# Weight-block sums: the low parts move to GpSimd, the first sum waits, and the order is computed with later landings

## The chip, the cores and the metric

The kernel runs on one NeuronCore of a Trainium2 chip. The metric is the device time of one execution in microseconds (us); shorter is better. The engines are called as the profile calls them: PE is TensorE (matmuls, with PEld for its weight loads), DVE is VectorE, ACT is ScalarE, POOL is GpSimd, and SP is SyncE, whose queue issues the DMAs (SPq).

## What is computed

The reference is windowed attention with eight memory keys, and a feed-forward network on its result:

```python
# 4 batches x 8 heads x 768 queries, head size 64; chunks of 32 queries see 16 keys to the left, 8 to the right
scores = scale * np.matmul(q_c, k_full.transpose(0, 1, 3, 2))
a = np.exp(scores - np.max(scores, axis=-1, keepdims=True))
a = a / (np.sum(a, axis=-1, keepdims=True) + 1e-09)
out[:, :, c_start:c_end] = np.matmul(a, v_full)
...
# 3072 tokens x 512; w_in is 512 x 2048, w_out is 2048 x 512
h = x @ w_in
r = np.maximum(h, 0.0)
g = s * (r * r) + b
return (g @ w_out).astype(np.float32)
```

## The kernel before

**Number format.** Every large matrix product is done as three fp32r products: a value is held as a high part (a rounded copy) and a low part (the value less its high part), and low*high, high*low and high*high are added in PSUM. So each operand costs one ACT copy for the high part and one subtraction for the low part.

**Stages.** The 3072 tokens are eight chunks of 384. Chunks 0 to 3 go through the network as written: `hidden(u)` (line 564) multiplies one 128-wide slice of w_in with the chunk (12 matmuls, L571), ACT makes relu, square and affine of it and the high part gH (L579 to L582), DVE the low part gL (L583); `result(u)` (line 588, 9 matmuls, L596) multiplies gL and gH with the slice of w_out. There are 64 such steps u. Chunks 4 to 7 go through the network in pairs by a Strassen scheme (`mix`, `seven` with L769, `rest` with L884), which needs sums of weight blocks. In front of that and between the steps, the attention of each chunk and pair of heads runs: scores on PE (L426), a custom DVE operation for mask and maximum (L493), exp on ACT (L497), the norm on POOL with a reciprocal on DVE in its midst (L506, L508, L509), eight transposes of 32x32 blocks on DVE ("flips", L529), the product with the values on PE (L463).

**Weights.** The 32 slices of w_in and w_out are loaded and converted once from 64-bit words by `weight` (line 536): ACT L546 and L555, DVE L547, L549, L551 and L556. L556 writes the low part. The words come through a ring of four buffers (`words`), which the block sums and the loads of `mix` use later in the same ring, strictly in the order in which they were declared.

**Block sums.** `blocks(side, g)` (line 630) is called 16 times, for w_in (side 0) and w_out (side 1). For two slices it takes high and low together again on POOL (two L637 of 128x512), makes four sums and differences S1 to S4 of 128x256 from them (POOL: two L643, L645, L647), the high part of all four at once on ACT (L650) and their low part on DVE (L651, 128x1024). SP stores the parts to DRAM (L656, issued in the code of `put`), from where `seven` and `rest` stream them back. A block holds four buffers of the ring: `full`, `sums`, `high`, `low`.

**The order.** Nothing is issued in the order in which the Python code runs. `op` collects every operation with its engine, an assumed duration (`HOLD`), a priority and what it reads and writes; `Plan.lay` (line 169) lays them out by greedy list scheduling, and the result is issued as it stands, so each engine's queue has a fixed order. On the chip an instruction waits only for the data that it really uses. In the plan every block sum also depends on `all_w`, the parts of the last slice of either matrix, but the instruction for it reads only its own two slices. Operations marked `lock` on DVE and POOL are never laid over each other in the plan. A load is taken to land `LAND` = 2000 ns after its bytes have passed a wire of `RATE` = 400 bytes per ns.

Of the kernel before, what the change touches and what calls it, by code (L numbers as in the profile page):

```python
# [12 lines left out]
F32R = mybir.dt.float32r  # L13
# [3 lines left out]
ALU = mybir.AluOpType  # L17
# [24 lines left out]
NEARLY = 16  # L42
# [30 lines left out]
            low=475, affine_v=475, rec=120, max=212, flip=449, xlow=470, wlow=365, wjoin=610, wsign=612, out=600,  # L73
            small=300, prod=1062, half=525, gsum=985, gsumv=470, tsumv=850, one=180, chigh=420, scaled=400, add=480, wide=735, vsum=1260, ssum=700, shigh=950, slow=1143, tsum=1800, thigh=735, tlow=880, norm=1010, norm2=1870, wrest=1290, issue=440)
LATE = dict(PE=230, ACT=180, DVE=180, POOL=150, SP=0)
SAME = dict(PE=0, ACT=118, DVE=115, POOL=60, SP=0)
RATE, LAND = 400.0, 2000.0
SLOW, NSLOW = 290.0, 6
FLIGHT = 8
BEGIN = dict(PE=2500.0, ACT=2500.0, DVE=2500.0, POOL=2500.0, SP=800.0)  # L80


class Op:
    __slots__ = ("eng", "hold", "fn", "deps", "outs", "prio", "lock", "vals", "n", "start", "end", "left", "ready", "size", "done")


class Val:
# [55 lines left out]
class Plan:  # L143
# [5 lines left out]
    def op(self, eng, kind, prio, fn, reads=(), writes=(), lock=False, size=0):  # L149
        o = Op()  # L150
        o.eng, o.hold, o.fn, o.prio, o.lock, o.n, o.size = eng, HOLD[kind], fn, prio, lock, len(self.ops), size
        o.deps, o.outs, o.vals = set(), [], []
        for part in reads:
            o.deps.update(part[1])
        for part in writes:
            o.deps.update(part[1])
            o.deps.update(part[2])
        for part in reads:
            part[2].append(o)
        for part in writes:  # L160
            part[1][:] = [o]
            part[2].clear()
        o.vals = list({id(p[0]): p[0] for p in (*reads, *writes)}.values())
        for v in o.vals:
            v.left += 1
        self.ops.append(o)
        return o

    def lay(self, filler=None):

        for o in self.ops:
            o.left, o.ready, o.start = len(o.deps), 0.0, None
            for d in o.deps:
                d.outs.append(o)
        engines = ["PE", "ACT", "DVE", "POOL", "SP"]
        free = dict(BEGIN)
        lock = {"DVE": 0.0, "POOL": 0.0}
        waiting = {e: [] for e in engines}
        ready = {e: [] for e in engines}
        events = sorted(BEGIN.values())  # L180
        wire, flying, sent = 0.0, [], 0
        laid = []
        back = []
        for o in self.ops:
            if not o.left:
                heapq.heappush(waiting[o.eng], (0.0, o.n, o))
        todo = len(self.ops)
        while todo:
            t = heapq.heappop(events)
            while events and events[0] <= t:  # L190
                heapq.heappop(events)
            while back and back[0][0] <= t:
                v = heapq.heappop(back)[-1]
                v.ring.back(v)
            for e in engines:
                while waiting[e] and waiting[e][0][0] <= t:
                    o = heapq.heappop(waiting[e])[2]
                    heapq.heappush(ready[e], (o.prio, o.n, o))
                if free[e] > t:
                    continue  # L200
                if e == "SP":
                    flying = [x for x in flying if x > t]
                    if len(flying) >= FLIGHT:
                        heapq.heappush(events, min(flying))
                        continue
                put, got = [], None
                while ready[e]:
                    x = heapq.heappop(ready[e])
                    o = x[2]
                    new = [v for v in o.vals if v.slot is None and v.ring.tiles is not None]  # L210
                    other = "POOL" if e == "DVE" else "DVE"
                    held = o.lock and e in lock and lock[other] > t

                    if o.lock and e in lock and free[other] <= t and any(y[2].lock and y[:2] < x[:2] for y in ready[other]):
                        put.append(x)
                        continue
                    given = []
                    for v in new if not held else ():
                        if not v.ring.can(v):
                            break  # L220
                        v.ring.give(v)
                        given.append(v)
                    if not held and len(given) == len(new):
                        got = o
                        break
                    for v in reversed(given):
                        v.ring.undo(v)
                    if held:
                        heapq.heappush(events, lock[other])
                    put.append(x)  # L230
                for x in put:
                    heapq.heappush(ready[e], x)
                if got is None:
                    if e == "PE" and filler and filler[0](t):
                        laid.append((t, -1, filler[1]))
                        free[e] = t + HOLD["warm"]
                        heapq.heappush(events, free[e])
                    continue
                o = got
                o.start = t  # L240
                free[e] = t + o.hold
                o.end = free[e] + LATE[e]
                if o.size:
                    wire = max(wire, t) + o.size / (RATE if sent >= NSLOW else SLOW)
                    sent += 1
                    o.end = wire + LAND
                    flying.append(o.end)
                if o.lock and e in lock:
                    lock[e] = free[e]
                laid.append((t, o.n, o.fn))  # L250
                todo -= 1
                heapq.heappush(events, free[e])
                for d in o.outs:
                    d.left -= 1
                    d.ready = max(d.ready, free[e] + SAME[e] if d.eng == e and not o.size else o.end)
                    if not d.left:
                        heapq.heappush(waiting[d.eng], (d.ready, d.n, d))
                        heapq.heappush(events, d.ready)
                for v in o.vals:
                    v.left -= 1  # L260
                    v.done = max(getattr(v, "done", 0.0), o.end)
                    if not v.left and v.ring.tiles is not None:
                        heapq.heappush(back, (v.done, o.n, o.vals.index(v), v))
                        heapq.heappush(events, v.done)
            if not events and todo:
                stuck = [(o.eng, o.prio, [v.kind for v in o.vals if v.slot is None]) for e in engines for _, _, o in ready[e]]
                raise AssertionError(f"the plan is stuck at {t}: {todo} left, {stuck[:12]}")
        self.end = max(o.end for o in self.ops)
        laid.sort(key=lambda x: (x[0], x[1]))
        return laid  # L270
# [3 lines left out]
def body(ctx: ExitStack, tc: tile.TileContext, qkv, w1, w2, out):  # L274
    nc = tc.nc
# [5 lines left out]
    op = plan.op  # L281
# [31 lines left out]
    words = ring("words", 4, [P, 2 * DM], F32)  # L313
# [29 lines left out]
    def warm():  # L343
        nc.tensor.matmul(idle, ones[:, :P], ones, start=True, stop=True)
# [285 lines left out]
    def blocks(side, g, due):  # L630

        fs = (2 * g, 2 * g + 1)
        parts = [[c_w[side, f]["H"], c_w[side, f]["L"]] for f in fs]
        full, sums, high, low = (Val(words) for _ in range(4))
        at = lambda v, i, n=1: v.tile[:, i * 2 * P:(i + n) * 2 * P]
        for k, f in enumerate(fs):
            op("POOL", "vsum", due, lambda k=k, f=f: nc.gpsimd.tensor_tensor(  # L637
                at(full, 2 * k, 2), weight_tile(side, f)[:, 0].bitcast(F32), weight_tile(side, f)[:, 1].bitcast(F32), ALU.add),
               [*parts[k], *all_w], (full[k],), lock=True)
        whole = (full[0], full[1])  # L640
        a12, a21 = (2, 1) if side else (1, 2)
        for i, a, b, how in ((0, a21, 3, ALU.add), (2, 0, a21, ALU.subtract)):
# [5 lines left out]
           (*whole, sums[1]), (sums[3],), lock=True)  # L648
        every = [sums[i] for i in range(4)]
        op("ACT", "shigh", due, lambda: nc.scalar.activation(high.tile.bitcast(F32R), sums.tile, AF.Copy), every, (high[0],))  # L650
        op("DVE", "slow", due, lambda: nc.vector.tensor_tensor(low.tile.bitcast(F32R), sums.tile, high.tile, ALU.subtract),  # L651
           (*every, high[0]), (low[0],), lock=True)
        for n, name in enumerate(BLOCKS):
            unit, q = divmod(ORDER2.index(name) * (NF // 2) + g if side else g * len(BLOCKS) + n, 2)
            dst = (w1s, w2s)[side][unit][:, q]
# [2 lines left out]
            if name in SUMS:  # L658
                i = SUMS.index(name)
                put(lambda i=i: at(high, i), dst[:, 0], (high[0],), 0)  # L660
                put(lambda i=i: at(low, i), dst[:, 1], (low[0],), 1)
            else:
                i, k = int(name[1]) - 1, int(name[2]) - 1
                if side:
# [286 lines left out]

    laid = plan.lay((lambda t: spare and t < 40e3, warm))
    with tc.manual_schedule():
        for _, _, fn in laid:
            fn()


# [37 lines left out]
```

## Time and profile before

| | |
|---|---|
| median of 3 runs | 618.76 us (618.1 to 619.36) |
| the profiled execution | 621.25 us, of which 619.5 us are the span |
| mean granted TensorE clock | 0.997 |
| PE busy | 598.3 us (97%) |
| DVE busy | 456.2 us (74%) |
| ACT busy | 435.1 us (70%) |
| POOL busy | 188.9 us (30%) |

The span runs from the first to the last instruction. Busy shares are means over stages with different limits, so the stages have to be read one by one. In a timeline row, the bracket at the end gives the idle time of that engine just before the row and what ended it. A matmul's end is modelled, so PE shown as busy can still be a little short of its peak.

### The profile page before, as it was taken

The page shows a single profiled execution, that of the slowest core. Times are in us where ns is not written, and L with a number is a line of the kernel's source. Part 1 is how long each engine was busy: PE and PEld are TensorE (multiplying, and loading weights), DVE is VectorE, ACT ScalarE, POOL GpSimd, SP SyncE. Part 2 cuts the span into 40 slices and gives each one's busy share as a digit, 9 for nine tenths or more (in the row PEclk, how much of TensorE's full clock was granted, in tenths as well). Part 3 has the DMA queues.
Part 4 walks back from the last instruction along what each step waited for, and adds up shares of the span by engine and source line. Part 5 has one row for each costly group of instructions (what it writes and reads, how often), then busy time and mean ns, then how long its engine had stood idle before and what let it go on. Part 6 is the DMA issues. An engine that isn't in the chain of part 4 may idle for free.

```text
span 619.5 us, 11570 instructions
## 1 busy us (share of the span) xinstructions
PE 598.3 (97%) x3827; PEld 539.0 (87%) x3831; DVE 456.2 (74%) x1277; ACT 435.1 (70%) x1157; POOL 188.9 (30%) x202
## 2 busy tenths in 40 slices
PE   9999999899999899999999999999999999999996
PEld 5778778788888788887878789999999999999996
DVE  5999899856787877776765778784999544439873
ACT  6999998675766888668585767775765436656562
POOL 4623100568575577683112022321000001110000
PEclk9999999899999999999999999999999999999999
DMA  8934665034887989789435648787878887777871
GB/s 332 404 130 157 204 220 172 1 115 136 275 246 250 304 256 277 253 268 312 123 118 199 219 141 300 250 296 249 266 245 285 292 283 251 243 248 252 274 225 52
DMA packets 68988, 141.28 MB, mean 228 GB/s; under 512 B 6976, under 2 KB 39744, under 8 KB 68928
## 3 DMA queue, kind: packets, MB, share of 16 engines
q1 hardware_dynamic: 68928, 140.54, 68.0%
q8 instruction: 30, 0.49, 0.3%
q14 instruction: 30, 0.25, 0.1%
HBM read 101.71 MB, written 38.80 MB: 227 GB/s over the span
## 4 chain that ended last, share of the span: by engine, by line
PE 56%; DVE 17%; ACT 12%; DMA 8%; issue 3%; SPq 3%; POOL 1%; ACTq 0%; DVEq 0%; POOLq 0%
PE ps L769 19%; PE ps L884 19%; PE ps L596 7%; PE ps L571 5%; ACT t L497 4%; DVE aT L529 3%; DVE gL L583 2%; PE ps L426 2%; DVE w L556 2%; DVE wv L551 2%; PE ps L463 2%; DMA words<-xs 2%; SPq L656 2%; DVE wv L549 2%; ACT words L650 1%
## 5 line engine op out<-in xcount | busy, mean ns | idle before, releaser
L571 PE MATMUL ps<-x,w 128*128 128x384 f32 x768 | 147.7, 339 | 0.5 <-DVE w L556 0.4
L571 PEld LDWEIGHTS ps<-x,w 128*128 128x128 f32 x768 | 135.2, 189 | 7.5 <-DVE w L556 0.9
L596 PE MATMUL ps<-w,gH 128*128 128x512 f32 x384 | 121.3, 397 | 0.2 <-DVE w L556 0.2
L497 ACT ACTIVATE t<-t,nmax 96x128 f32<-96x128 f32 x256 | 100.1, 396 | 29.4 <-DVE nmax L493 28.9
L769 PE MATMUL ps<-again,again 128*128 128x384 f32 x672 | 120.1, 338 | 0.0
L769 PEld LDWEIGHTS ps<-again,again 128*128 128x128 f32 x672 | 117.8, 188 | 1.0
L596 PE MATMUL ps<-w,gL 128*128 128x512 f32 x192 | 79.9, 416 | 13.8 <-DVE gL L583 13.8
L529 DVE STREAM_TRANSPOSE aT<-t 32x256 f32<-32x256 f32 x192 | 83.6, 435 | 11.1 <-POOL t L509 8.4
L509 POOL TENSOR_TENSOR t<-t,rden 96x1024 f32<-96x1024 f32 (+1 forms) x40 | 66.2, 1657 | 67.7 <-DVE rden L508 67.6
L596 PEld LDWEIGHTS ps<-w,gH 128*128 128x128 f32 x384 | 72.6, 189 | 14.7 <-ACT w L555 0.5
L884 PE MATMUL ps<-gH,again 128*128 128x386 f32 x272 | 70.2, 339 | 0.0
L493 DVE CUSTOM_DVE_ANT_0 t<-ps,mask 96x128 f32<-96x128 f32 x256 | 58.7, 281 | 15.3 <-PE ps L426 14.9
L596 PEld LDWEIGHTS ps<-w,gL 128*128 128x128 f32 x192 | 36.1, 188 | 27.2 <-DVE gL L583 19.0
L579 ACT ACTIVATE ps<-ps 128x384 f32<-128x384 f32 x64 | 30.6, 478 | 40.0 <-PE ps L571 39.4
L506 POOL TENSOR_SCALAR rden<-den 96x8 f32<-96x8 f32 (+1 forms) x40 | 12.1, 303 | 145.8 <-ACT t L497 145.2
L583 DVE TENSOR_TENSOR gL<-ps,gH 128x384 fp32r<-128x384 f32 x64 | 35.4, 553 | 24.4 <-ACT gH L582 23.3
L884 PE MATMUL ps<-again,again 128*128 128x386 f32 x264 | 50.1, 338 | 0.0
L497 ACT ACTIVATION_READ_ACCUMULATOR t<-t,nmax 96x1 f32 x256 | 49.8, 195 | 0.0
L884 PEld LDWEIGHTS ps<-gH,again 128*128 128x128 f32 x272 | 49.7, 189 | 0.0
L884 PEld LDWEIGHTS ps<-again,again 128*128 128x128 f32 x264 | 46.9, 189 | 0.0
L637 POOL TENSOR_TENSOR words<-w 128x512 f32<-128x512 f32 x32 | 46.4, 1469 | 0.6
L884 PE MATMUL ps<-gL,again 128*128 128x386 f32 x136 | 46.0, 339 | 0.0
(100 smaller groups left out, 908.2 us busy)
## 6 DMA issues: line engine op xcount, KB each, us to landing
again<-w1s SPq DMA_DIRECT2D x56, 512.0 KB, 4.3
again<-w2s SPq DMA_DIRECT2D x56, 512.0 KB, 4.3
raw<-qkv SPq DMA_DIRECT2D x28, 448.0 KB, 4.1
words<-w SPq DMA_DIRECT2D x22, 512.0 KB, 4.1
w1s<-words SPq DMA_DIRECT2D x64, 128.0 KB, 2.2
w2s<-words SPq DMA_DIRECT2D x64, 128.0 KB, 2.2
v<-qkv SPq DMA_DIRECT2D x28, 256.0 KB, 4.2
w1s<-w SPq DMA_DIRECT2D x24, 256.0 KB, 3.3
```

Source lines behind the costliest of these rows:

```text
L426: nc.tensor.matmul(scv(n)[:, j, :], raw.tile[rows, j * QB:(j + 1) * QB], raw.tile[rows, TOK + j * P:TOK + (j + 1) * P], start=True, stop=True)
L493: op("DVE", "max", a + 0.1, lambda j=j: nc.vector.tensor_tensor_reduce(t.tile[:, n, j, :], scv()[:, j, :], mask[:, kind(j)], -SCALE, 3.0e3 ...
L497: op("ACT", "exp", a + 0.2, lambda j=j: nc.scalar.activation(t.tile[:, n, j, :], t.tile[:, n, j, :], AF.Exp, bias=nmax()[:, j:j + 1], scal ...
L509: op("POOL", "norm2" if wide else "norm", a + 0.25, lambda: nc.gpsimd.tensor_tensor(t.tile[:, heads], t.tile[:, heads], rden().unsqueeze(3 ...
L529: nc.vector.transpose(aT.tile[gg, :, :, cs], t.tile[cs, :, :, gg])
L571: nc.tensor.matmul(h.tile[:, :TOK], weight_tile(0, f)[:, wi, c * P:(c + 1) * P], x.tile[c][:, xi], start=(c == 0 and n == 0), stop=(c == N ...
L579: op("ACT", "relu", u - ahead, lambda: nc.scalar.activation(hp(), hp(), AF.Relu), (), (h[0],))
L583: op("DVE", "low", u - ahead, lambda: nc.vector.tensor_tensor(g.tile[1][:, :TOK], hp(), g.tile[0][:, :TOK].bitcast(F32), ALU.subtract), (h ...
L596: nc.tensor.matmul(acc.tile, g.tile[gi][:, t * P:(t + 1) * P], weight_tile(1, f)[:, wi, :], start=(first and n == 0), stop=(last and n == 2))
L637: op("POOL", "vsum", due, lambda k=k, f=f: nc.gpsimd.tensor_tensor(at(full, 2 * k, 2), weight_tile(side, f)[:, 0].bitcast(F32), weight_til ...
L769: nc.tensor.matmul(bank.tile[:, :TOK], w.tile[:, lo:lo + P], xv.tile[xi][:, kc], start=(not more and kc == 0 and i == 0), stop=(kc == 1 an ...
L884: nc.tensor.matmul(sx(bank), w.tile[:, lo:lo + P], cut.tile[xi], start=(first and k == 0), stop=(last and k == 2), skip_group_check=True)
```

## The change

Three things are changed. The low parts of the block sums are taken by POOL, in two halves of 128x512 and in place (written over `sums`), where DVE did it in one instruction into a fourth buffer; a block then holds three buffers of the ring. The very first block sum gets a real dependency on the instructions that write the low parts of the last slices, so that POOL waits for them on the chip. And in the plan, every load or store after the first 16 is taken to land 1600 ns plus its bytes times (1/190 - 1/400) ns after the wire in place of 2000 ns; the whole order is laid out anew with this.

```diff
@@ constants
 RATE, LAND = 400.0, 2000.0
+HOP, ALONE = 1600.0, 190.0
...
@@ Plan.lay
                     wire = max(wire, t) + o.size / (RATE if sent >= NSLOW else SLOW)
                     sent += 1
-                    o.end = wire + LAND
+                    o.end = wire + (LAND if sent <= NEARLY else HOP + o.size * (1 / ALONE - 1 / RATE))
                     flying.append(o.end)
...
@@ blocks
-        full, sums, high, low = (Val(words) for _ in range(4))
+        full, sums, high = (Val(words) for _ in range(3))
...
-            op("POOL", "vsum", due, lambda k=k, f=f: nc.gpsimd.tensor_tensor(
+            o = op("POOL", "vsum", due, lambda k=k, f=f: nc.gpsimd.tensor_tensor(
                 at(full, 2 * k, 2), weight_tile(side, f)[:, 0].bitcast(F32), weight_tile(side, f)[:, 1].bitcast(F32), ALU.add),
                [*parts[k], *all_w], (full[k],), lock=True)
+            if not (side or g or k):
+                o.after += [p[1][0] for p in all_w[1::2]]
...
         op("ACT", "shigh", due, lambda: nc.scalar.activation(high.tile.bitcast(F32R), sums.tile, AF.Copy), every, (high[0],))
-        op("DVE", "slow", due, lambda: nc.vector.tensor_tensor(low.tile.bitcast(F32R), sums.tile, high.tile, ALU.subtract),
-           (*every, high[0]), (low[0],), lock=True)
+        for k in range(2):
+            op("POOL", "vsum", due + 0.1, lambda k=k: nc.gpsimd.tensor_tensor(
+                at(sums, 2 * k, 2).bitcast(F32R), at(sums, 2 * k, 2), at(high, 2 * k, 2), ALU.subtract), (high[0],), every[2 * k:2 * k + 2], lock=True)
...
-                put(lambda i=i: at(low, i), dst[:, 1], (low[0],), 1)
+                put(lambda i=i: at(sums, i), dst[:, 1], (sums[i],), 1)
...
@@ body, where the laid order is issued
-        for _, _, fn in laid:
-            fn()
+        for _, _, o in laid:
+            if o is None:
+                warm()
+                continue
+            o.ins = o.fn()
+            for x in o.after:
+                tc.add_manual_dep(o.ins.ins, x.ins.ins.name, mybir.DependencyInfo(mybir.DependencyClass.Sync, mybir.DependencyReason.DATA))
```

## Rows read from the trace of the kernel before

**Rows 1.** The page's part 1: busy time, share of the span, instructions.

```profile
PE 598.3 (97%) x3827; PEld 539.0 (87%) x3831; DVE 456.2 (74%) x1277; ACT 435.1 (70%) x1157; POOL 188.9 (30%) x202
```

**Rows 2.** Stretches: length, busy PE, PEld, DVE, ACT, POOL (instructions), PE clock, DMA.

```profile
118.00:285.00 167.00, 159.91 (x1048) 139.14 (x1049) 119.25 (x362) 120.14 (x347) 112.76 (x117) 0.99 0.72 231
285.00:365.00 80.00, 75.47 (x504) 64.79 (x503) 56.32 (x189) 57.67 (x174) 13.62 (x13) 1.00 0.54 180
365.00:615.00 250.00, 249.69 (x1516) 245.99 (x1514) 173.34 (x387) 150.57 (x323) 26.21 (x25) 1.00 0.76 252
```

**Rows 3.** Waits of PE, 121 to 290 us: total, times, longest.

```profile
PE ps L596 <- DVE gL L583: 6.3, 6, 1.8
```

**Rows 4.** Timelines of DVE, POOL and PE around the end of the weight conversions.

```profile
112.57 1.70 DVE L556 TENSOR_TENSOR w<-wv,w 128x512 fp32r<-128x512 f32 x1
114.20 1.78 DVE L551 SCALAR_TENSOR_TENSOR wv<-words,wv 128x512 int32<-128x512 int32 x1
117.25 0.69 DVE L556 TENSOR_TENSOR w<-wv,w 128x512 fp32r<-128x512 f32 x1
...
112.43 3.00 POOL L637 TENSOR_TENSOR words<-w 128x512 f32<-128x512 f32 x2
...
119.93 0.50 PE L596 MATMUL ps<-w,gL 128*128 128x512 f32 x1 [2.46 <-DVE gL L583]
```

**Rows 5.** The stretch right behind the stall; columns as in rows 2.

```profile
120.00:125.00 5.00, 5.00 (x17) 4.28 (x18) 2.01 (x7) 0.92 (x4) 3.17 (x4) 0.66 0.00 0
```

**Rows 6.** The line of the low parts: duration ns min/median/max, first and last start.

```profile
L651 DVE TENSOR_TENSOR words<-words,words x16: 1210/1298/4049, 130.6 to 284.8; 128x1024 fp32r<-128x1024 f32 x16
```

**Rows 7.** DVE's groups, 118 to 285 us: busy us, mean ns, idle before.

```profile
L529 DVE STREAM_TRANSPOSE aT<-t 32x256 f32<-32x256 f32 x93 | 40.5, 435 | 4.2 <-POOL t L509 2.9
L651 DVE TENSOR_TENSOR words<-words,words 128x1024 fp32r<-128x1024 f32 x16 | 32.5, 2033 | 10.1 <-ACT words L650 10.1
```

**Rows 8.** Timelines of ACT, DVE, POOL and PE around one low part.

```profile
179.51 0.49 ACT L582 ACTIVATE gH<-ps 128x384 fp32r<-128x384 f32 x1
...
178.46 3.48 DVE L651 TENSOR_TENSOR words<-words,words 128x1024 fp32r<-128x1024 f32 x1 [0.84 <-ACT words L650]
181.87 0.54 DVE L583 TENSOR_TENSOR gL<-ps,gH 128x384 fp32r<-128x384 f32 x1
...
179.56 3.53 POOL L637 TENSOR_TENSOR words<-w 128x512 f32<-128x512 f32 x2
...
182.46 0.50 PE L596 MATMUL ps<-w,gL 128*128 128x512 f32 x1 [0.87 <-DVE gL L583]
```

**Rows 9.** POOL's L637, then its groups, 112 to 285 us.

```profile
L637 POOL TENSOR_TENSOR words<-w x32: 1267/1298/2308, 112.4 to 274.6; 128x512 f32<-128x512 f32 x32
...
L637 POOL TENSOR_TENSOR words<-w 128x512 f32<-128x512 f32 x32 | 46.4, 1469 | 0.6
L509 POOL TENSOR_TENSOR t<-t,rden 96x1024 f32<-96x1024 f32 x13 | 25.0, 1925 | 39.4 <-DVE rden L508 39.4
```

**Rows 10.** Timelines of POOL, DVE and PE around one late norm.

```profile
357.89 1.90 POOL L509 TENSOR_TENSOR t<-t,rden 96x1024 f32<-96x1024 f32 x1 [0.47 <-DVE rden L508]
...
359.82 2.68 DVE L529 STREAM_TRANSPOSE aT<-t 32x256 f32<-32x256 f32 x6 [1.64 <-POOL t L509]
...
363.15 0.50 PE L596 MATMUL ps<-w,gL 128*128 128x512 f32 x1 [0.59 <-DVE gL L583]
```

**Rows 11.** DMA issues: count, KB each, median us to landing.

```profile
raw<-qkv SPq DMA_DIRECT2D x28, 448.0 KB, 4.1
words<-w SPq DMA_DIRECT2D x22, 512.0 KB, 4.1
```

**Rows 12.** Waits for landed loads; PE's from 290 us; a piece of the chain.

```profile
ACT again L718 <- DMA words<-xs: 5.8, 3, 3.8
...
PE ps L596 <- DVE gL L583: 3.3, 3, 1.5
...
309.76 5.57 DMA words<-xs
```

More of the change, by code (lines that the diff above doesn't have):

```diff
@@ L83 @@
 class Op:
-    __slots__ = ("eng", "hold", "fn", "deps", "outs", "prio", "lock", "vals", "n", "start", "end", "left", "ready", "size", "done")
+    __slots__ = ("eng", "hold", "fn", "deps", "outs", "prio", "lock", "vals", "n", "start", "end", "left", "ready", "size", "done", "after", "ins")
 class Val:
@@ L151, in op @@
         o.eng, o.hold, o.fn, o.prio, o.lock, o.n, o.size = eng, HOLD[kind], fn, prio, lock, len(self.ops), size
-        o.deps, o.outs, o.vals = set(), [], []
+        o.deps, o.outs, o.vals, o.after, o.ins = set(), [], [], [], None
         for part in reads:
@@ L234, in lay @@
                     if e == "PE" and filler and filler[0](t):
-                        laid.append((t, -1, filler[1]))
+                        laid.append((t, -1, None))
                         free[e] = t + HOLD["warm"]
@@ L249, in lay @@
                     lock[e] = free[e]
-                laid.append((t, o.n, o.fn))
+                laid.append((t, o.n, o))
                 todo -= 1
```

## The prediction

> **What bounds the kernel now.** I read the page's busy shares first: PE is at 97% of the span [rows 1], so what can be won is PE's idle time, not the time of any other engine. Then the stretches. From 365 to 615 us PE is busy 249.69 of 250 us [rows 2]: that part is PE's own work, and the time is set by how late it begins. In front of it PE lacks 7.1 us from 118 to 285 (167.00 less 159.91) and 4.5 us from 285 to 365 (80.00 less 75.47). In those stretches no other engine is full: DVE is busy 119 of 167 us, ACT 120, POOL 113. So PE's idle time there is made by the order in the queues, not by throughput, and the third view to read is who PE waits for. It has one answer: 6 waits with 6.3 us for gL of L583 from 121 to 290 us [rows 3], and 3 with 3.3 us behind that [rows 12]. One more, the longest, stands at the end of the weight conversions: 2.46 us [rows 4].
>
> **The entry of the block sums.** The first pair of L637 starts at 112.43 and runs to 115.43, while DVE still converts the last weights [rows 4]. The plan has the sums behind all conversions, but on the chip nothing held POOL. In those 3 us two conversions of DVE took 1.70 and 1.78 us; the next L556 took 0.69, and the two stood for 2 x 0.69 otherwise, so 2.1 us were lost. They are in front of the gL for which PE then waits 2.46 us. Behind the wait the granted clock is 0.66 over 5 us [rows 5], between the two levels 1.2 and 2.4 GHz: 5 x 0.34 = 1.7 us more. With the added dependency POOL can't start before the last L556 has ended (117.25 + 0.69 = 117.94, less 2.1 = 115.8). The 2.1 us go, 0.36 us of wait stay, and I take the dip of the clock to go with the long idle time ahead of it: 3.8 us. Bounds: 0, if the new order has something else in front of that gL, and 2.46 + 1.7 = 4.2. What queues behind the waiting sum on POOL are the other sums and the next norm; the sums begin 3.4 us later (115.8 less 112.43), which costs nothing as long as they end before the loads of `mix`, below.
>
> The Trainium skill, SBUF — State Buffer, section "Who interferes with whom", says that a DVE instruction with two SBUF inputs and a GpSimd instruction that reads SBUF share a port, and that whichever starts second is blocked until the first ends. The two stretched conversions agree with it. By this rule alone the low parts would from now on meet no DVE instruction of that kind from 118 to 285 us, and the sum would be the one below.
>
> **The low parts leave DVE.** L651 runs 16 times, 1210 ns at the fastest, 4049 at the slowest [rows 6], 32.5 us in sum with a mean of 2033 [rows 7]. What that costs PE is seen at one of them: gH is done at 179.51 + 0.49 = 180.0, L651 holds DVE from 178.46 to 181.94, gL follows at 181.87, and PE starts 0.87 us late at 182.46 [rows 8]. Without L651 gL would have stood 1.9 us earlier, and the wait is gone. Of the six waits of rows 3, five have an L651 right ahead of the gL, or ahead of the transposes and maxima that delay its gH; in the sixth gH itself comes late. So I count five sixths of 6.3 us, 5.3 us. Bounds: 0, if other work moves into the same place, and 6.3. The wider reason for taking most of it: DVE has 32.5 of its 119 us less from 118 to 285.
>
> **The low parts come to POOL.** They are 32 instructions of 128x512, two inputs, like L637, whose median is 1298 ns [rows 9]; the subtraction isn't in the trace, nor the fp32r output on POOL. Bounds are L637's fastest and slowest, 1267 and 2308; I take the median, as no DVE work is left here that stretches them: 32 x 1.30 = 41.6 us. L637 itself would go from a mean of 1469 back to 1298: 32 x 0.17 = 5.5 us less. POOL from 118 to 285 then has 112.8 + 41.6 - 5.5 = 149 us plus the 5 us of sums that now start behind 115.8: 154 of 169 us, 91%. POOL becomes the fullest engine beside PE in this stretch, in place of DVE. The sums fit in time: behind 115.8, 154 us of work end at 270 us if POOL never waits, and some 15 us later if it does. (Without the 25.0 us of the 13 norms [rows 9], that is 129 us, or 8.1 us for each of 16 blocks.) The loads of `mix`, next on the ring, stand in the chain that ended last at 309.76 us [rows 12]. That a block holds three buffers of four helps here: the next `full` needn't wait for the stores of the old low parts.
>
> What POOL's load costs is the wait for norms. A norm's L509 stands ahead of eight transposes of L529, and these ahead of a gL on DVE. One such case shows the price: POOL's norm holds DVE up for 1.64 us, and PE waits 0.59 us for the gL behind it [rows 10]. So about 1.1 us of lateness is hidden, and what exceeds it is paid. A norm that meets one pair of low parts or sums (2 x 1.30 = 2.6 us) would cost 2.6 - 1.1 = 1.5 us. Bounds: none of the 13 norms of the stretch [rows 9], 0, and all, 19.5 us. Now there are 2.9 us of such waits on DVE in the stretch [rows 7], hardly any of it PE's; at 91% instead of 68% (112.76 of 167) I take two norms more that are late by a whole pair: 3.0 us lost.
>
> **The later landings.** The old plan had 512 KB land 524288/400 + 2000 = 3.3 us after the wire is free, the new one 4.4 us; for the 448 KB of `raw` it is 3.1 and 4.0. Measured are 4.1 and 4.1 [rows 11]: the new figures are nearer. The price of the old ones is what engines wait for loads: 5.8 us at L718 [rows 12], nearly all of it hidden from PE, except where a late load of `mix` makes the subtractions pile up ahead of one of the three gL of 3.3 us. The new order can move that either way; value 0, bounds 3.3 us won and as much lost.
>
> **The sum.** 621.25 (the profiled execution; 619.5 span and 1.75 around it) - 3.8 - 5.3 + 3.0 + 0 = 615.15. That execution is 2.49 us above the median of the runs, 618.76, and taken against this the forecast is 618.76 - 6.1 = 612.7 us, 1.0% less.
>
> **Rivals.** (a) *POOL sets the pace.* The place is the norm behind sums and low parts on POOL, with DVE's transposes waiting for it and gL behind them. At 1.5 us a norm the gain of 9.1 us is used up when six of the 13 are late by a pair; with eight it is 12.0 - 9.1 = 2.9 us slower: 621.7. For it speaks the 91%, and that the order is fixed, so that POOL can't catch up by taking a norm first. Against it: POOL stands idle for 54 of these 167 us now, more than the 36 us that it gets to do, and a late norm has been harmless up to 1.1 us.
>
> (b) *Half of it.* The entry stall goes, but what L651 cost comes back as POOL's waits: 618.76 - 3.8 = 615.0. The case for it is a low part that meets other DVE work as L651 met L637: it was 2033 - 1210 = 0.82 us a piece, 13 us in all, of which PE paid its 6.3. Against it, DVE's L529 has a mean of 435 ns with POOL busy two thirds of the time [rows 7], and no other DVE group of that stretch stands as stretched. In the Trainium skill, Perfetto Trace Analysis, section "Optimizing Scalar/DVE Operations", stands that moving work between DVE and GpSimd might not help, since the two share a port; that would be this rival.
>
> (c) *More than that.* The three waits of 3.3 us behind 290 go too, since loads are planned as they land, and no norm is late: 618.76 - 9.1 - 3.3 = 606.4.
>
> (d) *Nothing.* The newly laid order puts waits of the same size in other places, in the conversions or in `mix`: 618.8.
>
> **Chances.** The forecast, about 609.5 to 614.9, has 0.52; (b), 615 to 617.5, 0.18; (c) 0.06; (d) 0.06; (a) 0.18. A measurement of this kernel can tell about 0.2%, 1.2 us, from no change. Faster by more is the forecast, (b) and (c): 0.76. Within it is (d): 0.06. Slower is (a): 0.18. The range is 608.0 to 619.5: it takes in the forecast, (b), (d) and the near ends of (a) and (c), and leaves out most of (a) and half of (c).
>
> **What will show it.** Right, if the first L637 starts after the last L556, if the last two L556 and L551 take 0.7 us, if PE has no 2.5 us wait near 118 and the clock stays at 1.00 there; if no L651 runs on DVE and the 32 new POOL instructions take about 1.3 us; if PE's waits for gL from 121 to 290 us are about 3 us, and those that stay stand behind transposes that waited for L509. The last part, 250 us of full PE, should then start about 6 us earlier. Wrong, if POOL is idle for less than a tenth of the stretch and DVE waits for L509 by more than 10 us, or if the new order opens waits in the conversions before 118 us, where I count no change.

## The result and the profile after

The changed kernel takes 608.1 us (median of 4 runs, 607.2 to 610.8), the kernel before 618.8 in the same comparison: ratio 0.9835, 95% interval [0.9801, 0.9868], 10.2 us by the ratio. Forecast were 612.7 us, 6.1 less; the range began at 608.0, and the forecast's own band at 609.5. The page's part 1 after, beside [rows 1], and the two stretches of [rows 2] with the one of [rows 5]:

```profile
PE 594.8 (98%) x3831; PEld 538.0 (89%) x3831; DVE 425.8 (70%) x1261; ACT 435.3 (72%) x1157; POOL 223.9 (37%) x234
```

```profile
118.00:285.00 167.00, 165.90 (x1112) 144.92 (x1111) 94.91 (x362) 125.08 (x357) 151.06 (x153) 1.00 0.76 249
285.00:365.00 80.00, 77.95 (x522) 67.93 (x521) 58.10 (x201) 57.03 (x182) 15.50 (x15) 1.00 0.53 178
120.00:125.00 5.00, 5.00 (x27) 4.59 (x26) 2.47 (x6) 3.16 (x6) 4.83 (x6) 1.00 0.00 0
```

PE lacks 1.1 us from 118 to 285 where it lacked 7.1; DVE has 24 us less there and POOL 38 more; the clock behind the entry stays at 1.00. The work that PE does without a break in the end, the Strassen products, begins 11.6 us earlier. Their line before (L769) and after (L773), with the first and the last start behind the durations:

```profile
L769 PE MATMUL ps<-again,again x672: 333/337/449, 367.3 to 555.0; 128*128 128x384 f32 x168
```

```profile
L773 PE MATMUL ps<-again,again x672: 333/337/449, 355.7 to 543.4; 128*128 128x384 f32 x168
```

The waits after, PE's from 121 to 290 us, PE's from 290 to 366, and DVE's for norms from 118 to 285:

```profile
PE ps L597 <- DVE gL L584: 1.0, 2, 0.6
...
PE ps L597 <- DVE gL L584: 2.0, 3, 1.0
...
DVE aT L530 <- POOL t L510: 9.5, 7, 2.5
```

The 6.3 us of [rows 3] are 1.0, the 3.3 of [rows 12] are 2.0. DVE waits for norms three times as long as before (2.9 us in [rows 7]), and PE hardly pays for it. The entry, in the timelines of DVE and POOL after, beside [rows 4]:

```profile
113.32 0.67 DVE L552 SCALAR_TENSOR_TENSOR wv<-words,wv 128x512 int32<-128x512 int32 x1
...
115.28 0.69 DVE L557 TENSOR_TENSOR w<-wv,w 128x512 fp32r<-128x512 f32 x1
...
116.05 2.54 POOL L638 TENSOR_TENSOR words<-w 128x512 f32<-128x512 f32 x2 [29.96 <-DVE w L557]
```

The first sum waits for the last conversion, no conversion there is stretched, and the pair of sums takes 2.54 us, not 3.00. POOL's groups from 112 to 300 us after, busy us and mean ns, beside [rows 9]:

```profile
L638 POOL TENSOR_TENSOR words<-w 128x512 f32<-128x512 f32 x32 | 41.6, 1306 | 31.1 <-DVE w L557 30.0 <-DMA w1s<-words 0.9
L655 POOL TENSOR_TENSOR words<-words,words 128x512 fp32r<-128x512 f32 x32 | 40.7, 1289 | 3.2 <-ACT words L653 3.2
```

Low parts cost 1289 ns each (1298 was taken), the sums went from 1469 to 1306. One thing is new and bad: a wait of PE in the conversions. Timelines of POOL, DVE and PE after:

```profile
83.80 2.29 POOL L510 TENSOR_TENSOR t<-t,rden 96x1024 f32<-96x1024 f32 x1 [11.06 <-DVE rden L509]
...
84.25 2.39 DVE L550 SCALAR_TENSOR_TENSOR wv<-wv,words 128x512 int32<-128x512 int32 x1
...
87.16 0.50 PE L597 MATMUL ps<-w,gL 128*128 128x512 f32 x1 [2.28 <-DVE gL L584]
```

The new order puts a norm here that stood at 110 us before. DVE's conversion starts 0.45 us after it, takes 2.39 us in place of 0.69, and ends 0.55 us after the norm (86.64 and 86.09); the gL behind it makes PE wait 2.28 us. All of PE's waits for gL up to 121 us, before and after:

```profile
PE ps L596 <- DVE gL L583: 4.2, 5, 2.5
...
PE ps L597 <- DVE gL L584: 3.1, 3, 2.3
```

So with the 2.46 us of the entry gone, PE's waits up to 121 us are only 1.1 us shorter.

### The profile page after: what moved, and what is told of

Its sections match the earlier page's. It is cut to its first block, busy times and chain, and to the rows that moved or that the text cites. A ratio compares the mean times of both kernels' runs of the same rounds, so it can differ in the third digit from the quotient of the medians.

```text
span 606.7 us, 11596 instructions
## 1 busy us (share of the span) xinstructions
PE 594.8 (98%) x3831; PEld 538.0 (89%) x3831; DVE 425.8 (70%) x1261; ACT 435.3 (72%) x1157; POOL 223.9 (37%) x234
## 4 chain that ended last, share of the span: by engine, by line
PE 53%; POOL 18%; ACT 11%; DVE 10%; issue 4%; DMA 3%; SPq 1%; POOLq 0%; ACTq 0%; DVEq 0%
PE ps L773 20%; PE ps L888 20%; PE ps L597 5%; POOL words L655 5%; POOL words L638 4%; PE ps L572 4%; ACT t L498 3%; POOL t L510 3%; POOL words L646 2%; DVE aT L530 2%; PE ps L427 2%; DVE gL L584 1%; PE ps L345 1%; POOL words L650 1%; PE ps L464 1%
## 5 line engine op out<-in xcount | busy, mean ns | idle before, releaser
L773 PE MATMUL ps<-again,again 128*128 128x384 f32 x672 | 120.1, 338 | 0.0
L773 PEld LDWEIGHTS ps<-again,again 128*128 128x128 f32 x672 | 117.8, 188 | 1.0
L638 POOL TENSOR_TENSOR words<-w 128x512 f32<-128x512 f32 x32 | 41.6, 1306 | 31.1 <-DVE w L557 30.0
```

The costliest lines, as they stand in the source:

```text
L638: o = op("POOL", "vsum", due, lambda k=k, f=f: nc.gpsimd.tensor_tensor(at(full, 2 * k, 2), weight_tile(side, f)[:, 0].bitcast(F32), weight ...
L773: nc.tensor.matmul(bank.tile[:, :TOK], w.tile[:, lo:lo + P], xv.tile[xi][:, kc], start=(not more and kc == 0 and i == 0), stop=(kc == 1 an ...
```

## The experiments

All were timed against the kernel before on their own chip; ratios are to it, with 95% intervals.

**The parts one by one.** The dependency alone, on the order of before:

```diff
+            if not (side or g or k):
+                o.after += [p[1][0] for p in all_w[1::2]]
```

> The kernel before with the dependency of the first block sum alone; the laid order is the one of before. Theory (the terms of the prediction hold one by one): the two conversions stretched to 1.70 and 1.78 us are at 0.7, PE's wait of 2.46 us near 118 and the dip of the clock behind it go, 3.8 to 4.2 us less, 614.6 to 615.0. Rival (the gain of 10.7 us comes from the new order, not from its parts): the wait only moves to the next gL, less than 1.5 us gained, and the block sums that start 3.4 us later give back the rest.

Measured: 0.9943 [0.9921, 0.9964], 3.5 us less. Timelines of DVE, POOL and PE:

```profile
112.63 0.68 DVE L557 TENSOR_TENSOR w<-wv,w 128x512 fp32r<-128x512 f32 x1
113.23 0.68 DVE L552 SCALAR_TENSOR_TENSOR wv<-words,wv 128x512 int32<-128x512 int32 x1
...
115.96 2.52 POOL L638 TENSOR_TENSOR words<-w 128x512 f32<-128x512 f32 x2 [3.44 <-DVE w L557]
...
117.89 0.50 PE L597 MATMUL ps<-w,gL 128*128 128x512 f32 x1 [0.36 <-DVE gL L584]
```

The two conversions are back at 0.68 us, PE's wait fell from 2.46 to the 0.36 us that were worked out, and the clock from 120 to 125 is 1.00. The later waits are those of before (6.3 us from 120 to 290). The wait went as forecast. The dip of the clock went from this place, but in this profiled run it stands elsewhere, behind another wait of PE:

```profile
200.04 0.59 PE L597 MATMUL ps<-w,gL 128*128 128x512 f32 x1 [1.85 <-DVE gL L584]
...
200.00:205.00 5.00, 4.96 (x17) 4.15 (x17) 3.60 (x16) 4.16 (x16) 0.46 (x3) 0.66 0.99 341
```

Its mean clock is 0.997, as that of before; in five of the seven runs of this kernel it is 0.999 or 1.000, so they seem to be without a dip.

The later landings alone, low parts still on DVE, no dependency:

```diff
-                    o.end = wire + LAND
+                    o.end = wire + (LAND if sent <= NEARLY else HOP + o.size * (1 / ALONE - 1 / RATE))
```

> The kernel before with the later landings in the plan alone. Theory: worth 0 to 3 us, most of it in the waits of PE from 285 to 365 us (3.3 us before, 2.0 in the changed kernel); L651 stays on DVE with its mean near 2.0 us, so PE's waits for gL from 121 to 290 stay near 6 us: 616 to 619. Rival (the new order does it): 5 us or more gained with L651 still on DVE and the sums still starting inside the conversions.

Measured: 0.9816 [0.9797, 0.9836], 11.4 us less: as much as the whole change. My theory fell here, by far. PE's waits from 122 to 290 us in this kernel, and its group of low parts on DVE:

```profile
PE ps L597 <- DVE gL L584: 1.1, 2, 0.6
```

```profile
L652 DVE TENSOR_TENSOR words<-words,words 128x1024 fp32r<-128x1024 f32 x16 | 26.4, 1651 | 5.0 <-ACT words L651 4.3 <-DMA w1s<-words 0.6
```

The low parts are still there, 26.4 us of them, but PE doesn't wait for them. One of them, in the timelines of ACT and DVE, beside [rows 8] and a row of POOL from the kernel before:

```profile
180.76 1.06 ACT L651 ACTIVATE words<-words 128x1024 fp32r<-128x1024 f32 x1 [0.98 <-POOL words L648]
...
185.09 1.21 DVE L652 TENSOR_TENSOR words<-words,words 128x1024 fp32r<-128x1024 f32 x1
186.23 0.55 DVE L584 TENSOR_TENSOR gL<-ps,gH 128x384 fp32r<-128x384 f32 x1
```

```profile
177.71 1.90 POOL L509 TENSOR_TENSOR t<-t,rden 96x1024 f32<-96x1024 f32 x1 [0.32 <-DVE rden L508]
```

Its high part is done at 181.8; it starts 3.3 us later, at the place that the order gives it, runs 1.21 us while POOL stands idle, and delays its gL by 0.16 us (that gH is done at 186.07). In [rows 8] DVE stood waiting for the high part, the low part started at once, in the midst of POOL's norm and 1.1 us ahead of its next pair of sums, took 3.48 us, and gL was behind it.

The entry changed as well, without any dependency. POOL, PE and the stretch behind, and PE's waits for gL up to 121 us:

```profile
106.87 3.98 POOL L638 TENSOR_TENSOR words<-w 128x512 f32<-128x512 f32 x2 [20.68 <-ACT ps L582]
...
110.24 0.50 PE L597 MATMUL ps<-w,gL 128*128 128x512 f32 x1 [0.81 <-DVE gL L584]
115.76 0.50 PE L597 MATMUL ps<-w,gL 128*128 128x512 f32 x1 [1.07 <-DVE gL L584]
...
120.00:125.00 5.00, 5.00 (x27) 4.50 (x26) 2.63 (x8) 2.99 (x8) 2.27 (x3) 1.00 0.00 0
```

```profile
PE ps L597 <- DVE gL L584: 4.9, 5, 2.3
```

The sums still start inside the conversions, but the one wait of 2.46 us has become two of 0.81 and 1.07, and the clock stays at 1.00. The wait of 2.3 us is the new one in the conversions (at 87 us, as in the changed kernel). From 290 to 366 us PE has no wait for gL left, where there were 3.3 us.

The low parts on POOL alone (in place, three buffers; old landings, no dependency):

```diff
-        op("DVE", "slow", due, lambda: nc.vector.tensor_tensor(low.tile.bitcast(F32R), sums.tile, high.tile, ALU.subtract),
+        for k in range(2):
+            op("POOL", "vsum", due + 0.1, lambda k=k: nc.gpsimd.tensor_tensor(
```

> The low parts on POOL, in place and in three buffers, with the old landings and without the dependency. Theory: PE's waits for gL from 121 to 290 us fall from 6.3 to about 1 us and the entry stall stays: 5 to 6 us less, 612.5 to 614. Rival of the prediction (POOL's norms come late): PE's waits in that stretch behind transposes are 3 us or more and the gain is under 3 us.

Measured: 0.9864 [0.9848, 0.9879], 8.4 us less. PE's waits from 120 to 290 us without the entry's 2.5, which stays as before, and those from 290 to 366:

```profile
PE ps L597 <- DVE gL L584: 1.0, 2, 0.6
...
PE ps L597 <- DVE gL L584: 1.7, 4, 0.6
```

The waits of [rows 3] fell by 5.3 us, as counted; those behind 290 fell by 1.6 too, and none came up for late norms.

The dependency and the low parts, old landings:

> The whole change without the later landings. Theory: the dependency and the low parts add up, 9 to 10 us less, 608.5 to 610, and PE's waits behind 290 us are near the 3.3 us of before. Rival (the landings are needed for the gain): 612 or more.

Measured: 0.9816 [0.9795, 0.9837], 11.4 us: these two parts do add up (3.5 + 8.4 = 11.9), without any later landing.

The dependency and the later landings, low parts on DVE:

> The later landings and the dependency, low parts still on DVE. If the parts add up: 0.9816 less 0.0057, 0.976 of before. If the low parts on POOL are what the whole change lives on: 0.99 or more. Between: the landings alone have left PE 1.1 us of waits from 118 to 290, so the dependency can only win in the conversions, where two instructions still stretch by 1.1 us each beside the first sums and PE waits 4.9 us in all: 0.978 to 0.982.

Measured: 0.9796 [0.9770, 0.9821]. So each of the two, low parts or landings, brings the dependency's kernel to about 0.98, and the third part on top brings nothing that these runs can tell: the whole change has 0.9835.

**Are true landings the cause, or is any other order better?** Three kernels on the code of before: landings too early, landings later without regard to size, and a change in the plan that says nothing about either.

```diff
-                    o.end = wire + LAND
+                    o.end = wire + (LAND if sent <= NEARLY else 1000.0)
...
-exp=386,
+exp=389,
```

The flat landings have 3000.0 in the first line. The second stands alone in one kernel, and on top of the later landings of the change in a fourth one.

> The kernel before with all loads and stores after the first 16 taken to land 1000 ns after the wire, the wrong way. Theory A (true landings in the plan are what helps): no gain or a loss, 621 to 626 beside a before of 621.6, PE's waits for gL from 118 to 290 us at 6 us or more. Theory B (the order of before is an unlucky one, and any new one puts L651 elsewhere): a gain of 3 us or more, with fewer L651 right ahead of a gL than the 12 from 118 to 290 us of before.

> The kernel before with all loads and stores after the first 16 taken to land 3000 ns after the wire, whatever their size. Theory A: close to the run with the later landings alone (ratio 0.982), since the big loads land as measured, and only the 128 KB stores too late. Theory B: some gain of any size from 0 to 2%, not tied to that one.

> The kernel before with the plan's duration of one exp instruction 389 in place of 386 ns, which says nothing on landings, sums or ports. Theory A: within 0.4% of before. Theory B: the order falls differently all the same, and the time moves by more than 0.4%, most likely to less than before, with PE's waits for gL from 118 to 290 us below the 8.8 us of before (2.46 at 119.93 and 6.3).

> The later landings alone, and the plan's duration of an exp instruction 389 in place of 386 ns, so that the order falls differently again. If later landings are the cause: 0.980 to 0.986 of before, PE's waits for gL from 122 to 290 us under 3 us. If the two kernels with later landings owe their 0.982 to one lucky order which both share: 0.990 to 1.000, with waits of 4 us or more.

Measured: too early 1.0039 [1.0022, 1.0057]; later and flat 0.9815 [0.9788, 0.9841]; another exp 0.9982 [0.9963, 1.0002]; another exp with the later landings 0.9800 [0.9773, 0.9828]. Three kernels of three with later landings gain 1.8 to 2.0%, also with the order stirred; two of two without don't. So the landings are a cause, and their size class by class isn't what matters. For the early landings Theory A was right in the time only: it wanted 6 us or more of waits for gL behind 118 us, and there are 3.8. Where the wrong way costs is seen in the waits for landed weights, of the kernel before and of the kernel with early landings, and in the last conversion of the latter:

```profile
ACT wv L546 <- DMA words<-w: 1.2, 3, 0.7
```

```profile
ACT wv L546 <- DMA words<-w: 7.6, 9, 1.5
...
123.86 0.69 DVE L556 TENSOR_TENSOR w<-wv,w 128x512 fp32r<-128x512 f32 x1
```

A plan that takes loads for landed puts their conversion at the head of ACT's queue, and everything behind it waits: 7.6 us here, and the last conversion is over at 124.6 us, where it was at 117.9 before. With later landings 0 to 0.6 us of such waits are left. But this is not the whole gain. PE's waits for gL from 120 to 290 us are 1.1 us with flat later landings and 2.1 with the stirred ones, 6.7 with the stirred exp alone, and 3.8 with the early landings, which are thus better than before in this stretch and lose in the conversions. How the landing of loads moves the low parts in DVE's queue was not traced further.

**The new wait in the conversions.** That norm (chunk 2, first pair of heads) is held back until the last weights are converted, in the plan and on the chip; once with the low parts on DVE, once in the changed kernel:

```diff
+           [r] + [t[x] for x in each] + (all_w if behind else []), [t[x] for x in each], lock=True)
+        if behind:
+            o.after += [p[1][0] for p in all_w[1::2]]
```

> The kernel of the run with later landings and dependency, low parts on DVE, and one norm of POOL more held back: that of chunk 2, first pair of heads, waits in the plan and on the chip for the last converted weights, as the first block sum does. In the run without this, POOL's 2.29 us norm stands over a DVE conversion at 84 us, which takes 2.39 in place of 0.69 us, and PE waits 2.28 us for the gL behind it. Theory (it is that collision): that wait goes, 1.7 to 2.3 us less, ratio 0.976. Rival (the conversions are full on DVE anyway, so the wait comes up again at a later gL): 0.979 to 0.982, with 3 us of waits of PE in the conversions as before.

> The changed kernel with the same norm held back. Theory: 1.7 to 2.3 us less than the changed kernel, ratio to before 0.979 to 0.980 where the changed kernel had 0.9835. Rival as in the run with the low parts on DVE. The two kernels of this pair also say again whether the low parts on POOL are worth anything beside the later landings and the dependency: if they are, this one is the faster.

Measured: 0.9808 [0.9781, 0.9835] with the low parts on DVE, 0.9779 [0.9748, 0.9809] in the changed kernel. In the latter, POOL's norm and the wait of PE that takes the place of the 2.28 us:

```profile
112.65 1.89 POOL L510 TENSOR_TENSOR t<-t,rden 96x1024 f32<-96x1024 f32 x1 [39.12 <-DVE w L559]
...
86.35 0.50 PE L599 MATMUL ps<-w,gL 128*128 128x512 f32 x1 [0.57 <-DVE gL L586]
```

The wait went from 2.28 to 0.57, as the theory said, and this is the fastest of the kernels by its ratio. That it beats the changed kernel isn't settled: the intervals overlap, and with the low parts on DVE the same edit went from 0.9796 to 0.9808. There PE's waits for gL up to 121 us fell from 3.1 to 1.4, but those behind rose from 1.1 to 2.4, and 0.5 us of another wait came up. That fits the rival of the expectation, that the wait comes up again at a later gL. Between the two of this pair the low parts on POOL are 0.3% ahead, in the pair without the edit 0.4% behind.

**POOL's load.** The changed kernel with each sum of 128x512 written twice:

```diff
+            op("POOL", "vsum", due, lambda k=k, f=f: nc.gpsimd.tensor_tensor(
+                at(full, 2 * k, 2), weight_tile(side, f)[:, 0].bitcast(F32), weight_tile(side, f)[:, 1].bitcast(F32), ALU.add),
+               [*parts[k], *all_w], (full[k],), lock=True)
```

> The changed kernel with each of the 32 sums of 128x512 on POOL done twice into the same buffer, 32 instructions and about 42 us of POOL more. POOL's 154 us become 196, more than the 169 of the stretch, and the last low part comes some 25 us later, near 308 us. If late norms are hidden from PE, as the changed kernel says (DVE waited 9.5 us for norms and PE 1.0 us for gL), the time stays within 0.5% of the changed kernel's (0.982 to 0.988 of before). If POOL sets the pace once it is full, as the first rival of the prediction has it: DVE's waits for norms 20 us or more, PE's for gL 5 us or more, and 0.990 or above.

Measured: 0.9823 [0.9790, 0.9856], no slower than the changed kernel. Its stretches, DVE's waits for POOL from 118 to 290, and PE's for gL from 122 to 290:

```profile
118.00:285.00 167.00, 165.44 (x1110) 144.33 (x1108) 94.10 (x356) 123.38 (x354) 163.14 (x158) 1.00 0.70 228
285.00:365.00 80.00, 78.49 (x527) 68.34 (x524) 56.86 (x203) 59.66 (x185) 41.77 (x41) 1.00 0.63 212
```

```profile
DVE rden L509 <- POOL rden L507: 19.9, 11, 3.1
DVE aT L530 <- POOL t L510: 18.3, 12, 3.4
...
PE ps L597 <- DVE gL L584: 1.6, 3, 0.9
```

POOL is full (163 of 167 us), DVE waits 38 us for it, PE 1.6 us for gL. DVE, at 94 of 167 us, has the time to wait. The chain that ended last seems to say otherwise; part 4 of the page, before and in the changed kernel:

```profile
PE 56%; DVE 17%; ACT 12%; DMA 8%; issue 3%; SPq 3%; POOL 1%; ACTq 0%; DVEq 0%; POOLq 0%
...
PE 53%; POOL 18%; ACT 11%; DVE 10%; issue 4%; DMA 3%; SPq 1%; POOLq 0%; ACTq 0%; DVEq 0%
```

The chain now runs through POOL for 18% of the span. With the sums doubled it is 17%, and the time is no longer, so standing in that chain doesn't yet cost time.

## Why the prediction was right, and where not

**The bound was read rightly.** PE's own work sets the end, and only its waits in front of 365 us can be won. These went from 9.6 us (6.3 and 3.3) to 3.0 behind 121 us, and the start of the last part moved by 11.6. With the waits up to 121 us PE waited 13.8 us for gL before and 6.1 after; these 7.7 us and the 1.7 of the clock are 9.4, against 10.2 measured.

**The entry was right in its wait, and open in its clock.** Forecast 3.8 us, measured 3.5 by itself (95%: 2.2 to 4.9), with the remaining wait of 0.36 us to the digit. That the 1.7 us of the clock go with this wait isn't shown: the profiled run of the dependency alone has the same dip at 200 us. The prediction counted no change in the conversions before 118 us and named a wait opened there as a sign of being wrong. It came, 2.28 us: the same wait near 87 us stands in the runs with the later landings alone and with the dependency (2.26 and 2.28), and in none of the parts with the old landings, so it belongs to that term. The Trainium skill, SBUF — State Buffer, section "Who interferes with whom", fits here and at the new wait: of the DVE instruction with two SBUF inputs and the POOL instruction, the one that starts second ends after the first, by 0.55 us at either place (DVE at 115.98 and POOL at 115.43 in [rows 4], 86.64 and 86.09 after).

**The low parts were right as a count and too small as a sum.** 5.3 us of PE's waits were to go and went, in the run with the low parts alone, which gained 8.4. The 3.0 us set against them failed: the step "I take two norms more that are late by a whole pair: 3.0 us lost". Norms did come late, 9.5 us in place of 2.9, and twice that with POOL full, but PE's waits stayed at 1.0 and 1.6 us. The price of 1.1 us hidden and the rest paid came from a single late norm at 358 us; from 118 to 285 us DVE is idle for 72 us in the changed kernel, and a wait for a norm can fall into these. With this, rival (a) falls as well: POOL at 98% of that stretch set no pace. The prediction's sign for it, POOL idle for less than a tenth of the stretch and DVE waiting more than 10 us for norms, was all but there in the changed kernel (16 of 167 us, and 9.5) and wholly with the doubled sums, and no time was lost: it was a poor sign. Rival (b) asked for DVE work that the low parts on POOL would stretch, and there was none of note: all 32 ran at 1.29 us, and DVE's transposes, 435 ns each before, were no slower:

```profile
L530 DVE STREAM_TRANSPOSE aT<-t 32x256 f32<-32x256 f32 x98 | 42.7, 436 | 11.0 <-POOL t L510 9.5
```

**The later landings failed as a term.** The step was "value 0, bounds 3.3 us won and as much lost"; alone they measured 11.4 us less. Both the value and the bounds were taken from waits for loads and from the waits of PE behind 290 us. What the landings change is larger than the waits that name them: the whole order behind, and with it where 16 low parts stand in DVE's queue against gL. Won behind 290 us were just the 3.3 us of the bound, all of them, in the runs with the later landings alone and with the dependency. Not in the bounds were 5.2 us from 121 to 290 and the entry's dip of the clock. The two edits are then two ways to be rid of the same 5 us of waits.

**The sum was right by its parts' overlap.** Alone the parts are worth 3.5, 8.4 and 11.4 us, 23.3 in sum; together 10.2. Adding terms, as the prediction did, would with the right terms have missed by 13 us. PE's waits for gL show where the parts overlap (us in three stretches, from the profiled run of each kernel):

| kernel | to 121 | 121 to 290 | 290 to 366 | ratio |
|---|---|---|---|---|
| before | 4.2 | 6.3 | 3.3 | 1 |
| dependency | 1.5 | 6.3 | 2.7 | 0.9943 |
| low parts | 3.7 | 1.0 | 1.7 | 0.9864 |
| later landings | 4.9 | 1.1 | 0 | 0.9816 |
| dependency, low parts | 1.5 | 0.9 | 3.1 | 0.9816 |
| dependency, landings | 3.1 | 1.1 | 0 | 0.9796 |
| all three | 3.1 | 1.0 | 2.0 | 0.9835 |
| dependency, landings, norm held back | 1.4 | 1.7 | 0.7 | 0.9808 |
| all three, norm held back | 1.5 | 0.8 | 1.1 | 0.9779 |

From 121 to 290 us either the low parts or the landings win nearly all that there is, and the other adds nothing; behind 290 us the landings alone win more than with the low parts on POOL. These waits aren't the whole time: with early landings there are 10.8 us of them, fewer than before, and the kernel is no faster. The time lies in the range, but under the forecast's own band (609.5 to 614.9), and it came there by luck: one term at zero that was worth 11 us by itself, and two terms that it overlaps, made up for each other.

**Open:** by which loads or stores the later landings move the order so; whether the low parts on POOL are worth anything beside the other two parts (one pair of runs says 0.4% worse, the other 0.3% better, all within their intervals; the waits in the table have the same signs, 6.1 against 4.2 us and 3.4 against 3.8); and whether holding back the norm is a gain.

## What to carry to other kernels

Where an order is planned ahead and then fixed, a wrong assumption on one kind of instruction shows as waits elsewhere: correct the plan's latencies against the trace first, for a wait that looks like the fault of a slow instruction may be one of its place in the queue. Before counting two edits as two gains, ask whether they remove the same wait. And an engine that is nearly full isn't yet a bound: ask what slack the engine has that waits for it.

## What the runs showed of the hardware

A wait of PE of 2.46 us was followed by a granted clock of 0.66 over 5 us in the kernel before [rows 5], and one of 2.46 us by the same 0.66 in the run with the low parts alone:

```profile
119.50 0.50 PE L597 MATMUL ps<-w,gL 128*128 128x512 f32 x1 [2.46 <-DVE gL L584]
...
120.00:125.00 5.00, 5.00 (x19) 4.39 (x19) 2.01 (x7) 0.87 (x3) 3.61 (x5) 0.66 0.00 0
```

A wait of 2.28 us in the changed kernel left it at 1.00 (85 to 90 us), while another of 2.28 us, in the run with flat landings, went with 0.75 from 115 to 120 us:

```profile
85.00:90.00 5.00, 2.84 (x13) 2.44 (x14) 5.00 (x19) 3.79 (x11) 1.09 (x1) 1.00 0.29 107
...
113.74 0.50 PE L596 MATMUL ps<-w,gL 128*128 128x512 f32 x1 [2.28 <-DVE gL L583]
...
115.00:120.00 5.00, 5.00 (x21) 4.37 (x20) 4.85 (x12) 4.28 (x16) 1.35 (x2) 0.75 0.00 0
```

And the wait of 1.85 us that goes with 0.66 in the run with the dependency alone stands in the kernel before too, with 1.00 around it:

```profile
203.64 0.50 PE L596 MATMUL ps<-w,gL 128*128 128x512 f32 x1 [1.85 <-DVE gL L583]
...
200.00:205.00 5.00, 3.15 (x17) 2.61 (x16) 4.95 (x23) 3.37 (x11) 3.48 (x4) 1.00 0.86 304
205.00:210.00 5.00, 5.00 (x50) 4.30 (x49) 2.22 (x5) 4.76 (x16) 1.84 (x3) 1.00 0.94 313
```

The length of the wait alone doesn't decide it.
